# One pool of 2-KB slots for the early tiles, one-hot rows expanded on chip, query copies on VectorE

## The chip, the cores and the metric

The kernel runs on one core of a Trainium2 chip. The metric is the device time of one execution in microseconds. TensorE (PE) multiplies, VectorE (DVE), ScalarE (ACT) and GpSimd (POOL) work on tiles, SyncE (SP) and also ACT and POOL issue DMA transfers. Each engine takes its instructions in the order in which the program gives them and waits, at each, for what that instruction needs.

## The reference

Two layers follow each other: an attention that selects chunks of keys, and a two-layer MLP. The sizes are 4 batches, 8 heads, 768 positions, head size 64; the MLP takes 3072 tokens of 512 features through 2048.

```python
k_chunks = k.reshape(B, H, nc, chunk, D)              # chunk 32, nc 24
k_min, k_max = k_chunks.min(axis=3), k_chunks.max(axis=3)
ub = np.sum(np.maximum(q[:, :, :, None, :] * k_min[:, :, None, :, :],
                       q[:, :, :, None, :] * k_max[:, :, None, :, :]), axis=-1)
ub = np.where(pos[:, None] // chunk >= np.arange(nc)[None, :], ub, -1e9)
top_chunks = np.argsort(ub, axis=-1)[..., -6:]
scores = np.where(selected_and_causal, q @ k.T / np.sqrt(D), -1e9)
attn = softmax(scores)
x = (attn @ v).transpose(0, 2, 1, 3).reshape(B * S, H * D)
h = x @ w_in
out = (np.maximum(h, 0) + np.log1p(np.exp(-np.abs(h)))) @ w_out
```

Inputs and output are float32 in DRAM; the kernel multiplies in bfloat16.

## The kernel before, in words

The work is cut into 12 blocks of 256 queries (4 batches of 3 blocks each). Block n is prepared (`prep`), attended one pair of heads at a time (`attend`, four pairs), and sent through the MLP (`mlp_h`, then `mlp_y`).

*Preparation.* Keys and queries come with features on the partitions. `kx` holds the minimum and the maximum of every chunk of keys (L483, or L499 from the second batch on), `bd` (L516) places them so that one matmul against the positive part of the queries (`qp`) and one against the negative part (`qn`, both L554) gives the bound of every chunk (L575, L576). VectorE adds the causal mask (L582), finds the eight largest (L591) and writes for each query which chunks are below the sixth (L599, L602) to `mr`. This mask is transposed and becomes 32 further rows of the query operands: `qa` (64 feature rows and 32 mask rows, for the first head of a pair) and `qb` (for the second head). `qa`'s feature rows are copied from `qb` at L558: by POOL for the first three blocks, by VectorE afterwards.

*One-hot rows.* The key operands `ka` and `kb` have 32 rows that answer to the mask rows: one-hot rows, the same for every pair, which say to which chunk a key belongs and carry the large negative number. `c_ohb` builds them once in `ohb` (32 x 768): VectorE fills the tile (L317) and POOL cuts it with three selects (L305, L307, L309). A DMA issued by POOL (L324, in `background`) repeats them into `ka`, another into `kb`, 192 KB each, for each of the two buffers of `ka` and `kb`. The score matmul of L676 then adds the mask as it multiplies, and waits for these rows.

*Attention.* `attend` multiplies keys by queries (L676), ACT takes the exponential (L685), POOL clears what lies above the diagonal (L691), PE multiplies by v (L701), VectorE divides (L710, L722), and the result goes transposed into X (L730 and L735 for the first three blocks, a DMA transpose at L738 afterwards).

*The ramp.* The first three blocks (`NRAMP`, one batch) are handled otherwise than the rest, since nothing can hide them: PE transposes their keys and queries (L476, L535), ACT copies these from PSUM (L480, L539), and `ramp_loads` (L364) issues their 18 loads, two tiles each of k, q and v per block, 256 KB a tile, in pieces (L375 for k and q, L372 for v). Most are SP's; some of block 0's are ACT's. POOL casts their v tiles at L648. While PE has nothing to do in the ramp it multiplies zeros (L340)[...]; the planner puts these fillers in until its own time 30.

*Buffers.* A raw tile (`xf`, 128 x 512 float32, 2 KB a partition) has 8 buffers. After the ramp, casts go to `kq` (4 buffers of 2 KB, L445), DMA transposes to `kt` (2) and `mt` (2), and attention results to `oall` (2), each a pool of its own. After the ramp no more than four `xf` are in use (kind `l`).

*Weights.* w_in and w_out come as four chunks each by DMAs that POOL issues (L392, L395). `ORDER` says that they come after the loads of blocks 0, 1 and 2; `hold_pool` (L401) makes POOL wait for one tile named by `HOLD`, ("q", 1): block 2's second q tile. The loads of block 3 and later wait for the third w_out chunk (`LGATE`, a small DMA of SP's at L407).

*Who sets the order.* `Graph.schedule` is a planner that runs when the program is built. Every task has an engine, a duration, a priority and the tiles it reads and writes; the planner simulates the engines, the buffers and the DMA queues, and the order in which it starts the tasks is the fixed program order of every engine. In its DMA model (L155, L176) a queue gets a share by its packet size (`pkt`) plus 3 where others are busy. A task may have a second engine (`alt`), which the planner takes if it is free first; `port=True` keeps VectorE and POOL off each other's shared port. So any change of a duration, of a pool or of a priority can change the order everywhere.

Of the kernel before, what the change touches and what calls it, by code (L numbers as in the profile page):

```python
# [9 lines left out]
F32 = mybir.dt.float32  # L10
# [7 lines left out]
CH = 32  # L18
# [3 lines left out]
QB = 256  # L22
# [10 lines left out]
NRAMP = 3  # L33
WARM = 30.0
# [10 lines left out]
HOLD = ("q", 1)  # L45
# [3 lines left out]
PSUM_CAP = {"s": 3, "h": 3, "y": 2, "o": 2, "t": 3, "l": 4}  # L49


class Buf:
    def __init__(self, pool, kind=None):
        self.pool, self.kind, self.left, self.slot = pool, kind, 0, None
        self.held = {}
# [7 lines left out]
class Graph:  # L63
# [39 lines left out]
    def schedule(self):  # L103
# [44 lines left out]
        def flow(to):  # L148
            nonlocal moved
            while moved < to:  # L150
# [4 lines left out]
                slow = {id(q): q[0][2] if len(live) == 1 else q[0][2] + 3 for q in live}  # L155
# [16 lines left out]
        while True:  # L172
            nxt = events[0][0] if events else None
            live = [q for q in queues.values() if q]
            if live:
                total = sum(q[0][2] + (3 if len(live) > 1 else 0) for q in live)  # L176
                cand = moved + min(q[0][0] * total / q[0][2] for q in live)
                if nxt is None or cand < nxt:
                    nxt = cand
# [74 lines left out]
def build(nc, tiles):  # L254

    PE, AC, DV, PO, SP = nc and (nc.tensor, nc.scalar, nc.vector, nc.gpsimd, nc.sync) or (None,) * 5
    g = Graph({"ps": 8, "xf": 8, "kq": 4, "kt": 2, "qab": 6, "qpn": 4, "kx": 2, "ub": 2, "mr": 2,
               "mt": 2, "pt": 6, "st": 4, "oall": 2, "osb": 3, "x": 5, "g": 3, "e": 3, "yo": 2}, PSUM_CAP)
# [43 lines left out]

    def c_ohb():
        o = T("ohb")
        PO.affine_select(out=o, in_=o, compare_op=ALU.is_ge, fill=0.0, base=0,  # L305
                         channel_multiplier=-CH, pattern=[[1, S]])
        PO.affine_select(out=o, in_=o, compare_op=ALU.is_ge, fill=0.0, base=CH - 1,  # L307
                         channel_multiplier=CH, pattern=[[-1, S]])
        PO.affine_select(out=o, in_=o, compare_op=ALU.not_equal, fill=-1.0, base=-NCH,  # L309
                         channel_multiplier=1, pattern=[[0, S]])  # L310
# [5 lines left out]
    add("POOL", 0.45, c_identf, -10, w=["identf"], name="identf")  # L316
    add("DVE", 0.7, lambda: DV.memset(T("ohb"), NEG), -10, w=["ohb"], name="ohb0")  # L317
    add("DVE", 0.2, lambda: DV.memset(T("cmask"), 0.0), -9, w=["cmask"], name="cmask0")
    add("POOL", 2.5, c_ohb, -9, r=["ohb"], w=["ohb"], name="ohb")
    add("POOL", 0.35, c_cmask, -8, r=["cmask"], w=["cmask"], name="cmask")  # L320
    add("POOL", 0.45, c_ident, -7, w=["ident"], name="ident")
    def oh(which, i):
        dst = T("ka", i)[64:96] if which == "ka" else T("kb", i)[32:64]
        PO.dma_start(out=dst, in_=T("ohb").unsqueeze(1).to_broadcast([32, NP, S]))  # L324

    def background(i, pr, after):
# [576 lines left out]
```

## Time and profile before

| what | value |
|---|---|
| median of 4 runs | 265.21 us (265.0 to 265.6) |
| the profiled execution | 265.0 us |
| its span, first to last instruction | 263.3 us |
| TensorE's granted clock, mean | 0.996 |
| PE, ACT, DVE, POOL busy | 254.7, 202.4, 149.5, 91.8 us |
| DMA traffic | 40.03 MB, 152 GB/s over the span |
| zero matmuls (L340) | 134, 21.1 us |

The span is the time between the first and the last instruction; the execution has a little before and after it, 1.7 us here. "Busy" of PE is the union of pipelined matmuls, fillers included. A row of the profile's groups gives line, engine, operation, tiles (written<-read) with their shape and count, then busy time and the mean of one in ns, then the idle time of the engine before them and what ended it. A row of the view by windows gives busy time and number of instructions of each engine in that stretch, the granted clock, the DMA engines' share (it counts overlapping packets, so it passes 1) and the rate of the transfers. In a timeline, two instructions of one line that follow closely are merged ("x2").

### The profile page before, as it was taken

To read this page: it belongs to the slowest core of one execution; us is meant where nothing else is said; L and a number is where in the kernel's file an instruction comes from. 1 tells how busy PE (TensorE), PEld (TensorE's weight loads), DVE (VectorE), ACT (ScalarE), POOL (GpSimd) and SP (SyncE) were. 2 spreads that over 40 slices of the span, in tenths; PEclk is the share of its full clock that TensorE was granted. 3 is DMA by queue.
4 is the path that set the end of the run, shared out by engine and by line. 5 is a ranking of instruction groups with operands and counts; after the bars stand their busy time and mean duration, and the time that the engine had idled before them with its cause. 6 is when DMAs were issued, how large, how long until landed. Compare 5 with 4: busy or idle time off the path is not lost.

```text
span 263.3 us, 6794 instructions
## 1 busy us (share of the span) xinstructions
PE 254.7 (97%) x2594; PEld 191.8 (73%) x2594; DVE 149.5 (57%) x542; ACT 202.4 (77%) x366; POOL 91.8 (35%) x187
## 2 busy tenths in 40 slices
PE   8998999999979999999999999999999999999993
PEld 6797998777657677778668678668678778676751
DVE  7779676238389597729997766579263110210202
ACT  1795999987467977999679898949869789576650
POOL 7345763252327361346517172533201111100000
PEclk9999999999999999999999999999999999999998
DMA  8999999999994999999999997993213211130112
GB/s 158 212 200 210 178 208 196 207 184 223 217 239 98 211 256 179 247 196 235 153 212 224 198 239 147 208 194 80 40 47 79 41 44 40 39 83 0 42 40 80
DMA packets 121061, 40.03 MB, mean 152 GB/s; under 512 B 113668, under 2 KB 117764, under 8 KB 121028
## 3 DMA queue, kind: packets, MB, share of 16 engines
q1 hardware_dynamic: 113396, 33.83, 65.8%
q0 software_dynamic: 4480, 4.98, 11.2%
q10 hardware_dynamic: 3152, 0.79, 1.7%
q8 instruction: 20, 0.33, 0.5%
q14 instruction: 13, 0.11, 0.1%
HBM read 27.26 MB, written 6.29 MB: 127 GB/s over the span
## 4 chain that ended last, share of the span: by engine, by line
PE 80%; DVE 7%; DMA 6%; ACT 2%; issue 1%; SPq 1%; POOL 0%; DVEq 0%; ACTq 0%
PE ps L758 28%; PE ps L779 27%; PE ps L676 13%; PE ps L701 7%; DMA kt<-kq 3%; DMA xf<-in_v_dram 2%; PE ps L340 2%; DMA xf<-in_q_dram 1%; DVE qpn L554 1%; DVE kx L499 1%; PE ps L576 1%; SPq L438 1%; DVE bd L516 1%; ACT qab L539 1%; ACT kb L480 1%
## 5 line engine op out<-in xcount | busy, mean ns | idle before, releaser
L779 PE MATMUL ps<-w_out_sb,g 128*128 128x512 bf16 x384 | 106.3, 379 | 0.0
L758 PE MATMUL ps<-x,w_in_sb 128*128 128x256 bf16 x768 | 105.6, 272 | 0.2 <-DVE oall L722 0.2
L685 ACT ACTIVATE pt<-ps 128x512 bf16<-128x512 f32 (+1 forms) x192 | 92.9, 566 | 4.8 <-PE ps L676 4.1
L758 PEld LDWEIGHTS <-w_in_sb 128*128 128x128 bf16 x768 | 72.8, 98 | 24.7 <-issue 0.3
L764 ACT ACTIVATE e<-ps 128x512 f32<-128x512 f32 x96 | 57.3, 613 | 35.5 <-PE ps L758 35.1
L691 POOL TENSOR_SCALAR_AFFINE_SELECT pt<-pt 128x256 bf16<-128x256 bf16 x96 | 40.5, 428 | 102.8 <-ACT pt L685 102.8
L768 ACT ACTIVATE g<-e 128x1024 bf16<-128x1024 f32 x48 | 51.3, 1068 | 0.9
L779 PEld LDWEIGHTS <-g 128*128 128x128 bf16 x384 | 35.0, 98 | 13.9
L784 DVE COPY yo<-ps 128x512 f32<-128x512 f32 x24 | 16.5, 686 | 46.6 <-PE ps L779 46.4
L710 DVE RECIPROCAL st<-ps 128x4 f32<-128x4 f32 x48 | 8.4, 177 | 42.5 <-PE ps L701 29.6
L701 PEld LDWEIGHTS <-pt 128*128 128x128 bf16 x672 | 26.7, 97 | 5.3
L676 PE MATMUL ps<-qab,kb 128*128 128x256 bf16 x192 | 30.4, 259 | 0.2
L676 PE MATMUL ps<-qab,ka 96*128 96x256 bf16 x192 | 28.8, 258 | 1.5 <-DVE qab L641 1.5
L701 PE MATMUL ps<-v,pt 128*128 128x65 bf16 x672 | 28.3, 193 | 0.0
L445 POOL CAST kq<-xf 128x512 bf16<-128x512 f32 x36 | 22.4, 634 | 8.7 <-DMA xf<-in_k_dram 6.2
L499 DVE TENSOR_REDUCE kx<-kt 128x32 bf16<-128x1024 bf16 x18 | 21.5, 1211 | 4.9 <-DMA kt<-kq 4.8
L676 PEld LDWEIGHTS <-ka 96*128 96x128 bf16 x192 | 17.7, 97 | 8.2 <-issue 1.7
L340 PE MATMUL ps<-zero 128*128 128x256 bf16 x134 | 21.1, 289 | 1.1 <-DVE zero L344 1.1
L676 PEld LDWEIGHTS <-kb 128*128 128x128 bf16 x192 | 16.6, 97 | 5.5 <-DMA kb<-ohb 0.3
L443 POOL CAST v<-xf 128x512 bf16<-128x512 f32 x18 | 11.3, 631 | 15.6 <-DMA xf<-in_v_dram 15.5
L722 DVE TENSOR_TENSOR oall<-ps,st 128x256 bf16<-128x256 f32 x36 | 15.0, 420 | 0.8
L340 PEld LDWEIGHTS <-zero 128*128 128x128 bf16 x134 | 12.9, 104 | 2.9 <-DVE zero L344 1.1
(62 smaller groups left out, 186.4 us busy)
## 6 DMA issues: line engine op xcount, KB each, us to landing
out_dram<-yo SPq DMA_DIRECT2D x24, 256.0 KB, 2.9
xf<-in_v_dram SPq DMA_DIRECT2D x23, 256.0 KB, 5.1
xf<-in_k_dram SPq DMA_DIRECT2D x18, 256.0 KB, 4.3
xf<-in_q_dram SPq DMA_DIRECT2D x18, 256.0 KB, 4.8
w_in_sb<-in_moe_w_in_dram POOLq DMA_DIRECT2D x4, 512.0 KB, 8.5
w_out_sb<-in_moe_w_out_dram POOLq DMA_DIRECT2D x4, 512.0 KB, 13.0
xf<-in_k_dram SPq DMA_DIRECT2D x10, 128.0 KB, 5.2
xf<-in_q_dram SPq DMA_DIRECT2D x10, 128.0 KB, 3.9
```

The source lines that it names most:

```text
L340: PE.matmul(T(Fill)[:, 0:256], T("zero")[:, 0:128], T("zero"), start=True, stop=True)
L445: PO.tensor_copy(T(b_)[:, :, t], T(xf).rearrange("s (p c) -> s p c", p=NP))
L499: DV.tensor_reduce(T(kx)[:, m].rearrange("d p (t c) -> d p t c", t=NT), T(kt).rearrange("d (p t) (c s) -> d p t c s", t=NT, s=CH), axis=AX ...
L676: PE.matmul(T(sp)[:, z * QB:z * QB + QB - q0], kk[r0:r1, p, (j + z) * 128:(j + z + 1) * 128], qq[r0:r1, p, q0:QB], start=True, stop=True)
L685: AC.activation(T(pt)[:, j:j + 2].rearrange("k j c -> k (j c)")[:, 0:w], T(sp)[:, 0:w], ACT.Exp, scale=SCALE)
L691: PO.affine_select(out=diag, in_=diag, compare_op=ALU.is_ge, fill=0.0, base=0, channel_multiplier=-1, pattern=[[0, 2], [1, 128]])
L701: PE.matmul(o[:, u, h], T(pts[h])[:, j, c0:c0 + 128], T("v", i)[:, j, 2 * p + h, :], start=(j == 0), stop=(j == t0 + u))
L758: PE.matmul(o, T("w_in")[:, dt, ft * 128:(ft + 1) * 128], T(x)[:, dt], start=(dt == 0), stop=(dt == KDM - 1))
L764: AC.activation(T(e)[:, f2 * 2:f2 * 2 + 2].rearrange("f a s -> f (a s)"), T(hp), ACT.Exp)
L768: AC.activation(T(gb)[:, f4 * 4:(f4 + 1) * 4], T(e), ACT.Ln, bias=1.0)
L779: PE.matmul(T(y), T(gb)[:, f, u * 128:(u + 1) * 128], T("w_out")[:, f, :], start=(f == 0), stop=(f == KFF - 1))
L784: add("DVE", 0.6, lambda y=y, yo=yo: DV.tensor_copy(T(yo), T(y)), pr, r=[y], w=[yo], name=f"yo{n}")
```

## The change

Six things are edited.

- `xf`, `kq`, `kt`, `mt` and `oall` take their buffers from one pool `w2` of 18 slots of 2 KB; each sees a slot through its own view (`VIEWS`). Kinds keep the old numbers as caps for `kq`, `kt`, `mt`, `oall`, and 4 for the `xf` of later blocks. The ramp's `xf` have no cap.
- `HOLD` names block 2's first q tile.
- The one-hot rows are made of a small tile `eye` (32 x 24, POOL) which VectorE spreads over 32 columns for each chunk. For block 0's keys, ACT copies them into `ka` and `kb`, at a priority (`OHP`) between that of block 0's q and v loads; the DMAs of the first buffer carry blocks 1 and 2 alone. The score matmul waits for the rows of its own key block.
- The `qa` copies of the ramp go to VectorE.
- The v casts of the ramp may go to POOL or ACT.
- In the planner, a queue's share is by its packet size plus 1, the one-hot DMAs have another size and duration, and the set-up tasks other priorities.

```diff
+OHP = -98.5
+W2 = 18
...
-HOLD = ("q", 1)
+HOLD = ("q", 0)
...
-PSUM_CAP = {"s": 3, "h": 3, "y": 2, "o": 2, "t": 3, "l": 4}
+WIDE = {"xf", "kq", "kt", "mt", "oall"}
+PSUM_CAP = {"s": 3, "h": 3, "y": 2, "o": 2, "t": 3, "l": 4, "kq": 4, "kt": 2, "mt": 2, "oall": 2}
...
+        self.view = pool
+        if pool in WIDE:
+            pool, kind = "w2", kind or (pool if pool in PSUM_CAP else None)
...
-                slow = {id(q): q[0][2] if len(live) == 1 else q[0][2] + 3 for q in live}
+                slow = {id(q): q[0][2] if len(live) == 1 else q[0][2] + 1 for q in live}
...
-    g = Graph({"ps": 8, "xf": 8, "kq": 4, "kt": 2, "qab": 6, "qpn": 4, "kx": 2, "ub": 2, "mr": 2,
-               "mt": 2, "pt": 6, "st": 4, "oall": 2, "osb": 3, "x": 5, "g": 3, "e": 3, "yo": 2}, PSUM_CAP)
+    g = Graph({"ps": 8, "w2": W2, "qab": 6, "qpn": 4, "kx": 2, "ub": 2, "mr": 2,
+               "pt": 6, "st": 4, "osb": 3, "x": 5, "g": 3, "e": 3, "yo": 2}, PSUM_CAP)
...
+    def c_eye():
+        o = T("eye")
+        PO.memset(o, 0.0)
+        PO.affine_select(out=o, in_=o, compare_op=ALU.not_equal, fill=NEG, base=0,
+                         channel_multiplier=1, pattern=[[-1, NCH]])
+        PO.affine_select(out=o, in_=o, compare_op=ALU.not_equal, fill=-1.0, base=-NCH,
+                         channel_multiplier=1, pattern=[[0, NCH]])
+
     def c_ohb():
-        o = T("ohb")
...
+        DV.tensor_copy(T("ohb").rearrange("c (n s) -> c n s", s=CH), T("eye").unsqueeze(2).to_broadcast([32, NCH, CH]))
...
-    add("DVE", 0.7, lambda: DV.memset(T("ohb"), NEG), -10, w=["ohb"], name="ohb0")
-    add("POOL", 2.5, c_ohb, -9, r=["ohb"], w=["ohb"], name="ohb")
+    add("POOL", 0.5, c_eye, -12, w=["eye"], name="eye")
+    add("DVE", 0.86, c_ohb, -12, r=["eye"], w=["ohb"], name="ohb")
...
-    def oh(which, i):
-        dst = T("ka", i)[64:96] if which == "ka" else T("kb", i)[32:64]
-        PO.dma_start(out=dst, in_=T("ohb").unsqueeze(1).to_broadcast([32, NP, S]))
+    def oh(which, i, blks):
+        ks = slice(blks[0] * QB, (blks[-1] + 1) * QB)
+        dst = T("ka", i)[64:96, :, ks] if which == "ka" else T("kb", i)[32:64, :, ks]
+        return dst, T("ohb")[:, ks].unsqueeze(1).to_broadcast([32, NP, QB * len(blks)])
...
-            add("POOL", 0.6, lambda which=which: oh(which, i), pr, r=["ohb"], w=[(which + "c", i)],
-                name="oh" + which, after=after, dma=0.6, pkt=66, lat=0.7)
+            add("POOL", 0.6, lambda which=which: PO.dma_start(*oh(which, i, blks)), pr, r=["ohb"],
+                w=[(which + "c", i, k_) for k_ in blks], name="oh" + which, after=after, dma=0.8, pkt=200, lat=0.7)
...
-    background(0, -6, ())
+    for which in ("ka", "kb"):
+        add("ACT", 0.95, lambda which=which: AC.copy(*oh(which, 0, [0])), OHP, r=["ohb"], w=[(which + "c", 0, 0)],
+            name="oh" + which)
+    background(0, -6, (), [1, 2])
...
-            qe_, qd = ("POOL", 0.6) if ramp else ("DVE", 0.35)
-            add(qe_, qd, lambda sl=sl: (PO if ramp else DV).tensor_copy(T(qa)[0:64, sl], T(qb)[0:64, sl]), pr + 1.8,
+            add("DVE", 0.09 + 0.13 * len(hs), lambda sl=sl: DV.tensor_copy(T(qa)[0:64, sl], T(qb)[0:64, sl]), pr + 1.8,
                 r=[(qb, hh, z) for hh in hs for z in range(3)], w=[(qa, hh, 0) for hh in hs], port=True, name=f"qa{n}")
...
-                add("POOL", 0.55, lambda xv=xv, t=t: PO.tensor_copy(
-                    v_dst(n, t), T(xv).rearrange("s (h d) -> s h d", h=H)), pr + 2,
-                    r=[(xv, 0), (xv, 1)], w=[("v", i, blk * NT + t)], name=f"vc{n}")
+                def vc(eng, xv=xv, t=t):
+                    return lambda: (PO.tensor_copy if eng else AC.copy)(
+                        v_dst(n, t), T(xv).rearrange("s (h d) -> s h d", h=H))
+                add("POOL", 0.6, vc(1), pr + 2, r=[(xv, 0), (xv, 1)], w=[("v", i, blk * NT + t)], name=f"vc{n}",
+                    alt=("ACT", 0.52, vc(0)))
...
-                r = [(kn, i, j, hh), (kn, i, j + 1, hh), (kn + "c", i)] + ([("kb0", i)] if h else [])
+                r = [(kn, i, j, hh), (kn, i, j + 1, hh), (kn + "c", i, j // 2)] + ([("kb0", i)] if h else [])
...
-    background(1, BG, [landed["w_in", 3]])
+    background(1, BG, [landed["w_in", 3]], [0, 1, 2])
...
+VIEWS = {
+    "xf": lambda a: a.bitcast(F32),
+    "kq": lambda a: a.rearrange("s (p t c) -> s p t c", p=NP, t=NT),
+    "kt": lambda a: a.rearrange("d (j s) -> d j s", s=128),
+    "mt": lambda a: a.rearrange("d (p s) -> d p s", p=NP),
+    "oall": lambda a: a.rearrange("s (p t h d) -> s p t h d", p=NP, t=NT, h=2),
 }
```

## The prediction

> **What bounds the kernel now.** First the page's busy row and the filler's row, then the span cut in three (columns: length, busy time and instructions of PE, PEld, DVE, ACT and POOL, PE clock, DMA share, GB/s).
>
> ```profile
> PE 254.7 (97%) x2594; PEld 191.8 (73%) x2594; DVE 149.5 (57%) x542; ACT 202.4 (77%) x366; POOL 91.8 (35%) x187
> L340 PE MATMUL ps<-zero 128*128 128x256 bf16 x134 | 21.1, 289 | 1.1 <-DVE zero L344 1.1
> 0.00:31.00 31.00, 28.41 (x283) 24.38 (x284) 24.70 (x88) 20.09 (x40) 17.77 (x39) 1.00 1.07 191
> 31.00:259.30 228.30, 226.27 (x2313) 167.46 (x2311) 124.18 (x454) 182.35 (x327) 74.05 (x149) 1.00 0.76 147
> 259.30:263.30 4.00, 0.00 (x0) 0.00 (x0) 0.61 (x1) 0.00 (x0) 0.00 (x0) 0.76 0.34 131
> ```
>
> From 31 us to 259.3, PE lacks 2.03 us of being busy, 1.68 of it between 70 and 80. Before 31 it looks busy too, but 21.1 us is the zero matmul. So the span is a head of 31, a dense stretch, and a tail of 4 (last copy and store). The change adds and removes no real matmul: it can win only by starting the dense stretch earlier, and lose by opening holes in it.
>
> What ends the head? The same columns over the DMA stream, and the timelines of POOL, DVE and PE.
>
> ```profile
> 13.00:18.00 5.00, 5.00 (x64) 4.63 (x65) 3.78 (x14) 4.46 (x11) 2.68 (x7) 1.00 1.34 219
> 10.00:13.00 3.00, 2.91 (x32) 2.26 (x30) 2.17 (x14) 1.71 (x5) 1.79 (x3) 1.00 1.15 190
> 18.00:20.00 2.00, 2.00 (x25) 1.86 (x22) 1.82 (x7) 1.97 (x5) 0.68 (x3) 1.00 0.69 148
> 26.00:29.00 3.00, 3.00 (x33) 2.64 (x31) 2.97 (x9) 2.90 (x6) 3.00 (x5) 1.00 0.92 125
> 29.00:36.00 7.00, 7.00 (x103) 6.46 (x101) 3.37 (x13) 6.52 (x15) 5.67 (x12) 1.00 1.24 206
> ```
>
> ```profile
> 24.81 0.18 POOL L401 CAST scratch<-xf 1x1 bf16<-1x1 f32 x1 [2.81 <-DMA xf<-in_q_dram]
> 24.93 1.54 POOL L392 DMA_DIRECT2D w_in_sb<-in_moe_w_in_dram  x2
> ...
> 31.57 0.60 PE L758 MATMUL ps<-x,w_in_sb 128*128 128x256 bf16 x4
> ```
>
> The ramp's loads run at 219 GB/s, the weights at 206. POOL waits at L401 for block 2's second q tile and only then issues w_in. The first weight chunk needs 5.8 us to land (the shortest of that line's landings), 30.7, and the first MLP matmul runs at 31.57. X of block 0 was ready at 20.5 (its last copy, ACT L735 at 20.11, 0.37 long). The head is thus a DMA queue: 18 ramp tiles, then weights. The holes in it have names in SyncE's waits up to 32 us, for buffers not yet free:
>
> ```profile
> SPq L375 <- PE ps L576: 3.4, 1, 3.4
> SPq L375 <- POOL pt L691: 2.0, 1, 2.0
> ```
>
> Last, VectorE and GpSimd in the ramp:
>
> ```profile
> 19.84 1.64 DVE L516 COPY bd<-kx 64x64 bf16<-64x64 bf16 x2
> 19.92 0.61 POOL L558 COPY qab<-qab 64x512 bf16<-64x512 bf16 x1
> 20.84 0.60 POOL L558 COPY qab<-qab 64x512 bf16<-64x512 bf16 x1
> ```
>
> Two bd copies take 1.64 us while POOL copies qa; this copy's median is 0.178.
>
> **What the Trainium skill says.** "SBUF — State Buffer", section "SBUF: two separate sides": GpSimd and a VectorE operation in a two-port mode take an exclusive lock on one port pair, and the loser waits for the whole instruction. The bd row agrees: 1.46 for the longest, against 0.178. "DMA: Bandwidth & Descriptors", section "Queues, rings and completion order": each DMA engine goes round the queues that have work, packet by packet. So weights issued while ramp loads are queued get in between them; the trace of before hardly overlaps the two, and doesn't show the share.
>
> **The change, part by part.** Times are against the profiled execution (265.0, span 263.3, 1.7 around it).
>
> *Shared pool.* 18 ramp tiles fit 18 slots, so no ramp load waits for a buffer. Against 219 GB/s (206 for weights) the stream loses 3 x 29/219 = 0.40 us in 10:13, 2 x 71/219 = 0.65 in 18:20, 3 x 81/206 = 1.18 in 26:29. Sum 2.2. The last hole is partly the two block-2 v tiles issued late by SP (22.5), partly the late hold. I take all 2.2 as gained; at worst 1.2 (some of it may be the start-up of POOL's queue). In steady state the caps (4+4+2+2+2 = 14) are as before.
>
> *HOLD on q tile 0.* The hold opens a tile earlier: 262 kB/219 = 1.2 us. The weights then share with up to three ramp tiles; the bytes are the same. I take 0.4 for the first chunk (0 to 1.2), 0 for the end of the stream.
>
> *One-hot rows.* Block 0's rows go to two ACT copies, so the DMAs carry two thirds: 2 x 65.5 kB/219 = 0.6 us off the stream. The ACT copies have 1024 elements a partition: 1.07 each by the nearest row (L768, 128x1024, 1068 ns), 2.1 in all, inside ACT's idle 4.79 us before L480 at 6.88. Behind them on ACT stands block 0's second v load, issued at 4.80, perhaps 1 us later; its cast comes at 11.74 and the first AV matmul at 14.97, so about 2 us of cover. Gone, n=0 is later by up to 2.1, against X ready 11 us before use. Making the rows: POOL drops three selects of 0.815 (2.4) and adds a memset and two selects of 24 columns, under 0.3 each by the 128-column row (0.29); VectorE changes a 0.70 memset for a broadcast copy of 768, estimated 0.55 to 0.96 by "VectorE: DVE Perf Modes", section "The TRN2 errata — SBUF-src ops pay a fixed extra latency per instruction" (150 cycles plus 768, halved or not; no row of before has a broadcast copy). All before 5 us: nothing at the end.
>
> *qa copies to VectorE.* Six copies of 0.63 leave POOL. On VectorE I take 0.30 each (the qpn row of 128x512 is 0.316; 0.23 to 0.48 by the shortest qpn and the 64x1024 copy): 1.8, of which 1.2 falls before 26 us. It gives back 1.28 at bd and some 0.8 on four 128x256 qpn (0.43 mean against 0.226 shortest): net about -0.9 to +1.8, near zero taken, since DMA sets the end of the head. Queued behind these copies on VectorE are ub, max and mr of the same block.
>
> *v casts may go to ACT.* Up to six of 0.61 (L764's 128x512 row). Only four, 2.4 us, could fall where ACT is full: from 23 to 50 us it is idle 1.07.
>
> *The planner.* The queue penalty (3 to 1), durations and caps change the plan, so all static orders after the ramp may differ. The page can't price this; between -2.0 (the holes of the dense stretch closed) and +4; I take 0.
>
> Sum: first weight chunk 2.2 + 0.6 + 0.4 = 3.2 earlier (about 27.5, first MLP matmul at 28.4). The end of the weights, which releases the next loads (SP L407), is 2.8 earlier. PE's dense stretch needs both feeds, so the smaller counts: span 263.3 - 2.8 = 260.5, execution 262.2. The median of before is 0.2 above its profiled execution: 262.4.
>
> **Rivals.** A: *ScalarE becomes the bound.*
>
> ```profile
> 23.00:50.00 27.00, 27.00 (x348) 23.20 (x346) 17.40 (x85) 25.93 (x53) 14.12 (x27) 1.00 1.17 200
> ```
>
> ACT is as full as PE there. Only its idle stretch before L480 at 23.27 (2.78) can be filled; if two v casts also fall here (1.2) and the qa copies cost VectorE, and so block 1's first S, 0.7 net, 2.8 - 1.2 - 0.7 = 0.9 remains: 264.3. Against it: block 1's keys come earlier too.
>
> B: *the feed hole closes as well.* Between 70 and 80 us PE idles 1.68, waiting for block 4's kt. If the new plan orders SP's loads better, that and 0.3 besides goes: 260.4. For it: that hole is one load chain on SP; against: nothing in the diff speeds those transfers.
>
> C, *slower: SP's order.* SP issues loads, transposes and stores in one fixed order, and block 4's keys already come with no slack.
>
> ```profile
> 70.00:80.00 10.00, 8.32 (x85) 6.26 (x84) 7.51 (x20) 6.32 (x12) 3.28 (x7) 1.00 1.20 217
> ```
>
> A store put ahead of those loads, whose y tile is not finished, stops SP; store L788 waited 57.5 us in total, 11.6 at most, harmless late. A y tile is 16 matmuls of 512 columns, about 3.5 us of PE (two of the chain's 1.73 pieces of 8). One tile too early costs 3.5 and eats the gain; over 2.8 us it is slower. Two tiles, 7, less 2.8: about +4; I put the case at 267.5, between +0.7 and +4.
>
> D: *no change*, if the w_in landing is not what PE waits for: 265.2. Against it, X was ready 11 us before.
>
> **How the numbers follow.** Forecast 0.55 (own range 261.2 to 263.8), A 0.14, B 0.08, C 0.19, D 0.04. A change of 0.2% (0.53 us) is about what can be told here. Faster: forecast, B, most of A, 0.75; same: D and a bit of A, 0.06; slower 0.19. The range 259.8 to 266.6 takes in A, B, D and the near part of C; the worst of C and a low tail are left out.
>
> **What would show it.** No SP wait for PE or POOL in the ramp, and 219 GB/s held from 10 to 26 us. L401 ending near 22, the first L758 near 28.4, SP's L407 near 44, fewer fillers. No bd copy over 0.3 us in the ramp; block 0's S matmuls free of the kb<-ohb DMA. The dense stretch still about 228 long. I am wrong if L758 starts early and the hole at 70 to 80 has grown by as much (C), or if L758 starts early with ACT full and PE thin up to 50 (A), or if L401 still ends near 25.

## The result, and the profile after

The changed kernel takes 265.92 us (median; 264.43 to 269.12), the kernel before 264.99 in the same comparison: ratio 1.0037, 95% interval [1.0024, 1.005]. The ratio leaves out its two slowest executions (268.68 and 269.12), which lie over 1.5% above its fastest. It is slower by about 0.4%, where 262.4 was forecast. The profiled execution has a span of 264.0 us, against 263.3 before.

The page's busy row and the filler's row, then the span cut as in the prediction: head, dense stretch and tail, the DMA stream, and the stretches 23 to 50 and 70 to 140.

```profile
PE 254.7 (96%) x2593; PEld 191.9 (73%) x2593; DVE 146.2 (55%) x549; ACT 205.0 (78%) x369; POOL 85.0 (32%) x179
L355 PE MATMUL ps<-zero 128*128 128x256 bf16 x133 | 19.4, 287 | 1.1 <-DVE zero L325 1.1
```

```profile
31.00:260.00 229.00, 226.69 (x2310) 167.24 (x2308) 121.60 (x452) 182.37 (x329) 70.65 (x145) 1.00 0.71 144
260.00:264.00 4.00, 0.00 (x0) 0.00 (x0) 0.61 (x1) 0.00 (x0) 0.00 (x0) 1.00 0.35 131
10.00:13.00 3.00, 1.42 (x15) 1.26 (x16) 1.15 (x9) 2.91 (x7) 0.48 (x1) 1.00 1.15 260
13.00:18.00 5.00, 5.00 (x58) 4.25 (x56) 3.99 (x19) 4.00 (x9) 1.72 (x5) 1.00 1.11 248
18.00:20.00 2.00, 2.00 (x27) 1.85 (x25) 2.00 (x6) 1.94 (x5) 0.97 (x2) 1.00 0.57 129
23.00:26.00 3.00, 3.00 (x37) 2.81 (x35) 3.00 (x30) 2.55 (x5) 3.00 (x5) 1.00 0.71 97
23.00:50.00 27.00, 26.84 (x324) 22.97 (x322) 17.38 (x88) 26.11 (x53) 12.33 (x24) 1.00 1.15 199
70.00:80.00 10.00, 10.00 (x107) 7.75 (x106) 9.18 (x35) 7.72 (x15) 4.13 (x9) 1.00 1.06 198
80.00:90.00 10.00, 9.21 (x85) 6.20 (x84) 6.59 (x17) 7.70 (x14) 4.11 (x9) 1.00 0.81 142
120.00:140.00 20.00, 19.12 (x213) 13.77 (x211) 19.27 (x84) 14.31 (x29) 10.76 (x22) 1.00 1.04 212
```

Early loads run faster (248 to 260 GB/s), and the hole at 70 to 80 us is gone (PE 10.00 of 10). Two things are worse: PE is busy for only 1.42 of the 3 us from 10 to 13 (2.91 before), and it is thin at 80 to 90 and in 120 to 140. SyncE waits for no buffer in the ramp. Apart from the start of the program, its only wait up to 32 us is:

```profile
SPq L389 <- DMA w<-in_k_dram: 0.9, 1, 0.9
```

POOL's timeline around the hold (L415) and the first weights (start, length, "idle before"):

```profile
21.89 0.41 POOL L706 TENSOR_SCALAR_AFFINE_SELECT pt<-pt 128x256 bf16<-128x256 bf16 x1 [0.47 <-ACT pt L700]
22.25 0.18 POOL L415 CAST scratch<-w 1x1 bf16<-1x1 f32 x1
22.37 3.02 POOL L406 DMA_DIRECT2D w_in_sb<-in_moe_w_in_dram  x4
```

The DMA landings in the trace give four marks: w_in issued at 22.37 (24.93 before), first chunk landed at 28.54 (30.72), the last w_out chunk at 47.18 (49.78), SP's gate passed at 44.12 (46.70). The first MLP matmul runs at 29.99 (31.57). The hold did not wait for its tile: that tile's first piece had landed at 19.81, and the piece that the old hold reads at 20.84, while POOL came to the hold at 22.25, behind a select that had waited for ScalarE's exponential. So in this kernel it made no difference which of the two tiles the hold names.

So the stream did what was promised in direction and nearly in size. To see where the gain went I count the columns of all real matmuls (fillers left out) that have started by a moment, in units of 2400 columns (float32 columns count twice, and a matmul under 60 columns as 60); the whole is 229.35 in both kernels, and one unit is about one microsecond of the dense stretch (it advances 0.974 a microsecond from 140 to 255).

| by (us) | 15 | 31 | 60 | 80 | 90 | 130 | 135 | 255 |
|---|---|---|---|---|---|---|---|---|
| after minus before | -1.36 | +0.27 | -0.11 | +1.44 | +0.75 | +1.07 | -0.56 | -0.64 |

At 31 us, where the forecast had PE 2.8 ahead, it is 0.27 ahead: the first MLP matmuls come earlier, but there is less attention work done. The closed hole brings it to +1.44 at 80; it loses 1.6 between 130 and 135, and stays behind. Three questions follow: what holds the ramp back, why the earlier loads don't help later, and how much is the re-made plan.

ScalarE's timeline answers the first for a start. Of the kernel after, then of the kernel before:

```profile
3.65 0.38 ACTq L389 DMA_DIRECT2D w<-in_q_dram  x1
4.07 1.04 ACT L349 COPY ka<-ohb 32x1024 bf16<-32x1024 bf16 x1 [1.98 <-DMA w<-in_k_dram]
5.12 1.04 ACT L349 COPY kb<-ohb 32x1024 bf16<-32x1024 bf16 x1
8.99 0.38 ACTq L386 DMA_DIRECT2D w<-in_v_dram  x1
9.47 0.58 ACT L494 CAST ka<-ps 64x512 bf16<-64x512 f32 x1 [3.30 <-DMA w<-in_q_dram]
```

```profile
4.80 0.38 ACTq L372 DMA_DIRECT2D xf<-in_v_dram  x1
6.88 0.58 ACT L480 CAST ka<-ps 64x512 bf16<-64x512 f32 x1 [4.79 <-DVE kx L483]
```

The one-hot copies end at 6.16, in time. Block 0's second v load stands behind them, and it isn't issued until 8.99 (4.80 before), though its slot has been free from the start. The semaphore records of the trace say why. The loads of SP and ACT share eight semaphores, taken in turn in program order; a load waits until the transfer that had its semaphore last has landed. In the kernel before, the v load followed ACT's q load directly, and its turn fell on the semaphore of SP's second load (landed 4.78). After, seven loads of SP's stand between the two in the program, and the turn, having gone round once, falls on the semaphore of that q load itself: issued at 3.65, landed at 8.97. For 2.8 us ACT stands at a load, with the ka copy of L494 behind it. I call this *the stand*.

### The profile page after: what moved, and what is told of

Read it like the earlier page. It is cut to its first block, busy times and chain, and to the rows that moved or that the text cites. A ratio compares the mean times of both kernels' runs of the same rounds, so it can differ in the third digit from the quotient of the medians.

```text
span 264.0 us, 6800 instructions
## 1 busy us (share of the span) xinstructions
PE 254.7 (96%) x2593; PEld 191.9 (73%) x2593; DVE 146.2 (55%) x549; ACT 205.0 (78%) x369; POOL 85.0 (32%) x179
## 4 chain that ended last, share of the span: by engine, by line
PE 78%; DVE 10%; DMA 5%; ACT 4%; issue 2%; ACTq 0%; DVEq 0%
PE ps L794 26%; PE ps L773 26%; PE ps L691 13%; PE ps L716 7%; PE ps L355 4%; DVE kx L513 3%; DMA w<-in_q_dram 2%; ACT pt L700 2%; DMA w<-mr 1%; DMA w<-in_k_dram 1%; DVE mr L615 1%; DVE qpn L568 1%; DVE ub L604 1%; ACT e L779 1%; PE ps L589 1%
## 5 line engine op out<-in xcount | busy, mean ns | idle before, releaser
L799 DVE COPY yo<-ps 128x512 f32<-128x512 f32 x24 | 16.4, 685 | 48.2 <-PE ps L794 48.1
L716 PEld LDWEIGHTS <-pt 128*128 128x128 bf16 x672 | 26.6, 97 | 4.3
L716 PE MATMUL ps<-v,pt 128*128 128x65 bf16 x672 | 28.5, 193 | 0.0
L459 POOL CAST w<-w 128x512 bf16<-128x512 f32 x36 | 21.8, 625 | 11.4 <-DMA w<-in_k_dram 10.4
L513 DVE TENSOR_REDUCE kx<-w 128x32 bf16<-128x1024 bf16 x18 | 21.4, 1209 | 3.5 <-DMA w<-w 3.4
L355 PE MATMUL ps<-zero 128*128 128x256 bf16 x133 | 19.4, 287 | 1.1 <-DVE zero L325 1.1
L737 DVE TENSOR_TENSOR w<-ps,st 128x256 bf16<-128x256 f32 x36 | 15.1, 421 | 1.1
L457 POOL CAST v<-w 128x512 bf16<-128x512 f32 x18 | 11.0, 621 | 11.5 <-DMA w<-in_v_dram 11.5
```

The lines of the kernel that those rows point to most:

```text
L355: PE.matmul(T(Fill)[:, 0:256], T("zero")[:, 0:128], T("zero"), start=True, stop=True)
L459: PO.tensor_copy(T(b_)[:, :, t], T(xf).rearrange("s (p c) -> s p c", p=NP))
L513: DV.tensor_reduce(T(kx)[:, m].rearrange("d p (t c) -> d p t c", t=NT), T(kt).rearrange("d (p t) (c s) -> d p t c s", t=NT, s=CH), axis=AX ...
L716: PE.matmul(o[:, u, h], T(pts[h])[:, j, c0:c0 + 128], T("v", i)[:, j, 2 * p + h, :], start=(j == 0), stop=(j == t0 + u))
L799: add("DVE", 0.6, lambda y=y, yo=yo: DV.tensor_copy(T(yo), T(y)), pr, r=[y], w=[yo], name=f"yo{n}")
```

## The experiments

All are timed against the kernel before in five rounds. The edits act on the planner's finished order (`order`, a list of tasks that is then emitted) unless the diff says otherwise, and none leaves a part of the computation out. The diffs are shortened, some of them to words. A trace is of one execution; where two traces are compared, their landing times can differ by themselves: the first w_in chunk lands at 28.08 in one run below (e3) and at 26.45 in another (e7) that differs from it only from 50 us on.

### Parts of the change alone, in the kernel before

**The planner's price of a busy queue alone (e1).**

```diff
-q[0][2] + 3 for q in live          # both places
+q[0][2] + 1 for q in live
```

> The kernel before with one thing of the change alone: the planner's queue penalty 1 instead of 3. No operation is added or removed; only the order changes. Theory P (the plan decides: where the holes of the dense stretch fall moves the end by a microsecond either way, whatever the parts do): over 0.5 us away from before, with the holes between 60 and 140 us at other places. Theory S (the ramp decides, by ScalarE and its queue): within 0.5 us of before, since ScalarE's work is the same.

267.97 against 265.03, 1.0114 [1.007, 1.0158]. The re-made order alone costs some 1.1%, with PE 8.44 of 10 in 80 to 90 (9.82 before) and another hole at 150 to 160. My zero for the planner was no estimate.

**The slots alone (e2).** The order stays; early tiles take their buffer from 18 shared slots.

```diff
+    free = list(range(18))             # walk the order; each wide tile takes
+    b.slot = free.pop(0)               # the slot that came free first
```

> The kernel before, every engine's order kept, only the slots renamed: the five kinds of tiles share 18 slots, so no ramp load waits for a buffer. The forecast's step (2.2 us of holes in the DMA stream belong to the slots and the late hold, and pass to the end): the first w_in chunk lands 1 to 2 us before 30.7 and the time falls by 1 to 2 us. Theory S: w_in lands earlier, but PE and ScalarE are full from 31 us on, and the fillers are a fixed number, so the time falls by 0.5 us or less. If SyncE's waits were those of a window of outstanding DMAs and not of slots, w_in doesn't move at all.

265.98: 1.0018 [0.9994, 1.0043]. The first w_in lands at 30.04 instead of 30.72: 0.7 us, where 2.2 was counted for the slots. Even that need not be the slots' doing: in a run below that has the old buffers and the old hold (e13), it lands at 30.00. SyncE's issues hardly move; block 1's four q loads, before and in this run:

```profile
8.09 5.52 SPq L375 DMA_DIRECT2D xf<-in_q_dram  x4
8.08 5.37 SPq L378 DMA_DIRECT2D w<-in_q_dram  x4
```

The second of the four takes 3.69 us before and 3.50 here, and a later k load 2.52 and 2.51, although here no buffer is waited for. So what the waits showed as "for buffers" in the ramp had another limit beneath it. It isn't the turn of the eight semaphores either: the transfers that had the semaphores of these two loads last had landed at 8.26 and 13.84, before the issues began (8.80 and 15.25). What holds these issues stays open.

**The hold alone (e12).** The order stays; POOL's hold reads block 2's first q tile.

```diff
-tensor_copy(T("scratch")[0:1, 0:1], T(second q tile)[0:1, 0:1])
+tensor_copy(T("scratch")[0:1, 0:1], T(first q tile)[0:1, 0:1])
```

> The kernel before, every order kept, with POOL's hold on block 2's first q tile instead of the second. The forecast's step: the first w_in chunk lands 0.4 to 1.2 us before 30.7 and the time falls by up to that. Theory S (PE's and ScalarE's orders are fixed and both are full from 31 us on): w_in lands about 1 us earlier, the first MLP matmul 0.3 to 1 us, and the time stays within 0.4 us of before.

264.22: 0.9962 [0.9941, 0.9982], faster by 0.4%, but not as I had it. In the profiled execution the first w_in chunk lands no earlier (30.93), although issued 1.7 earlier (23.27): the last v tile of the ramp is still in the queue and lands at 31.25 instead of 28.36. That fits "DMA: Bandwidth & Descriptors" of the Trainium skill, section "Queues, rings and completion order", on queues served in turn. The first MLP matmul stays at 31.50. What moves is the feed of block 3: its first key tile lands at 51.73 instead of 53.13, its key transpose is issued at 53.82 instead of 55.04, and the hole at 70 to 80 shrinks by 1.0 (before: PE 8.32). Part of this may be chance, since with the old hold that tile lands at 52.57 (e13) and 52.65 (e2) in other runs; that the 0.4% comes from block 3's feed is likely, not shown.

```profile
70.00:80.00 10.00, 9.35 (x99) 7.22 (x98) 8.54 (x34) 7.44 (x14) 3.72 (x9) 1.00 1.15 208
```

### Undoing one thing in the changed kernel

**The v load first (e3).** Only block 0's second v load moves, ahead of ACT's two one-hot copies.

```diff
+    v = [t for t in order if t.name == "ldv01"][0]
+    order.remove(v)
+    order.insert(first_one_hot_copy_on_ACT, v)
```

> The changed kernel's order with one move: block 0's second v load stands on ScalarE's queue before the two one-hot copies, not behind them. Theory S: the load is issued near 4.8 us instead of 8.99, ScalarE's first ka copy runs near 7 instead of 9.47, block 0's first S matmul 2 to 2.6 us earlier, ScalarE has up to 2.6 us more to give before 31 us, and the time falls by 0.3 to 1.2 us. Theory P: block 0 is earlier, the holes stay, and the time stays within 0.3 us of the changed kernel.

264.19: 0.9967 [0.995, 0.9984]. One moved instruction turns +0.37% into -0.33%. ScalarE's timeline of this run:

```profile
4.28 0.37 ACTq L386 DMA_DIRECT2D w<-in_v_dram  x1
4.70 1.04 ACT L349 COPY ka<-ohb 32x1024 bf16<-32x1024 bf16 x1 [2.61 <-DMA w<-in_k_dram]
5.75 1.04 ACT L349 COPY kb<-ohb 32x1024 bf16<-32x1024 bf16 x1
6.82 0.58 ACT L494 CAST ka<-ps 64x512 bf16<-64x512 f32 x1
```

The one-hot copies themselves do fit: the ka copy comes at 6.82 (6.88 before). The move also lands the v tile earlier (10.30 for 12.47), but that is not what was missing: in the changed kernel block 0's v casts start at 12.52 and 12.84, and its first AV matmul (L716) runs at 17.23, behind the selects. The first MLP matmul is at 28.29, a little under the forecast 28.4, and PE is 1.87 units ahead at 31 us and 3.47 at 80. But by 135 the lead is 0.99, and in this profiled execution (span 263.3) nothing is left of it by 200 us; the median keeps 0.8 us of it.

**Other suspects in the changed kernel (e5, e6).** The last ten fillers dropped, which ran after w_in had landed; and, on top of the v load's move, two v casts taken off ScalarE:

```diff
-    order's last ten fillers                        # e5
-    v casts on ACT                                  # e6, e8
+    the same v casts on POOL
```

> The changed kernel's order without its last ten zero matmuls, those that ran between 28.5 and 30.1 us after the first weight chunk had landed (28.54). If the fixed number of fillers is what kept the earlier weights from PE: the first MLP matmul comes 1.1 us earlier and the time falls by 0.8 to 1.1 us. Theory S (ScalarE, full from about 20 to 50 us, sets the pace, and block 3's keys behind it): PE starts the MLP earlier, ScalarE doesn't, block 3's key transpose stays at 55, and the time falls by 0.4 us or less.

> The v load first, as in the run with that one move, and besides the two v casts that the plan gave to ScalarE (blocks 0 and 1, 0.62 and 0.65 us) done by POOL at the same places. Theory S: ScalarE gets 0.6 to 1.3 us back before 31 us, block 3's key transpose is 0.5 to 1 us earlier than the 53.3 of that run, and the time is 0.2 to 0.9 us below it. Theory P: no change over 0.2 us.

Fillers: 265.95, 1.004 [1.0025, 1.0055], as with them; the first MLP matmul comes at 29.30, 0.7 earlier, and the time doesn't follow. v casts: 264.38, 0.9959 [0.994, 0.9978], as without that edit (0.9967). The two casts, 0.64 us each on ACT, cost nothing that can be told.

**The feed of block 3 (e7, and with the v casts e8).** Its keys land 4.1 us earlier than before (the second tile at 50.15, before 54.27), and yet its key transpose is issued at the same time, 55.00 (55.04). POOL's timeline of the kernel after, then of the kernel before:

```profile
51.43 0.61 POOL L459 CAST w<-w 128x512 bf16<-128x512 f32 x1
54.01 0.41 POOL L706 TENSOR_SCALAR_AFFINE_SELECT pt<-pt 128x256 bf16<-128x256 bf16 x1 [1.97 <-ACT pt L700]
54.37 0.61 POOL L459 CAST w<-w 128x512 bf16<-128x512 f32 x1
```

```profile
52.20 0.41 POOL L691 TENSOR_SCALAR_AFFINE_SELECT pt<-pt 128x256 bf16<-128x256 bf16 x1 [1.45 <-ACT pt L685]
53.19 0.61 POOL L445 CAST kq<-xf 128x512 bf16<-128x512 f32 x1 [0.58 <-DMA xf<-in_k_dram]
54.32 0.61 POOL L445 CAST kq<-xf 128x512 bf16<-128x512 f32 x1 [0.52 <-DMA xf<-in_k_dram]
```

Before, the casts of the keys (L445) wait for DMA. After, the tiles are there, but a select of block 2 stands between the two casts and waits for ScalarE's exponential. ScalarE is busy for 26.11 of the 27 us from 23 to 50. So in this trace the earlier transfer is lost behind ScalarE. The test, on top of the v load's move:

```diff
+    second key cast of block 3 right after the first on POOL, ahead of that select
+    block 3's key transpose on SP moved up accordingly
```

> The v load first, and besides block 3's second key cast moved on POOL ahead of a diagonal select of block 2, which stood 1.97 us waiting for ScalarE's exponential, and block 3's key transpose right behind it on SyncE. Nothing changes on ScalarE, VectorE or PE. If that select is where the earlier weights and loads were lost (theory S, second half): the transpose is issued near 51 us instead of 53.3, block 3's chunk reductions near 57 instead of 59.2, and the time falls by 0.5 to 1.5 us against the run with the v load alone. If the feed of blocks 4 to 8 is set further down (by VectorE or the SyncE queue), block 3 is earlier and the time stays within 0.3 us.

> The changed kernel's order with all three moves: the v load first, the two v casts on POOL, block 3's key cast and transpose ahead. Theory S: the sum of the parts, 263 us or less against 265.0 of the kernel before and 265.9 of the changed one. Theory P: a hole elsewhere takes it back, and it is no faster than the v load alone (264.2).

The feed: 263.86, 0.9946 [0.9931, 0.9961], 0.2% below the v load's move alone, with intervals that overlap; so it isn't shown that this feed costs time. The transpose is issued at 51.0, but block 3's reductions on VectorE still start at 59.2, since VectorE's own order has the copy of a finished y tile (L799, 58.60) ahead. The part of the expectation that had them near 57 failed. With the v casts moved too: 263.94, 0.9957 [0.994, 0.9973]; nothing more.

### The hole at 130 to 135

PE's timeline of the kernel after shows the hole (last column: idle before, and its releaser):

```profile
132.88 0.20 PE L588 MATMUL ps<-bd,qpn 128*128 128x48 bf16 x1 [0.38 <-DVE qpn L568]
134.11 0.54 PE L691 MATMUL ps<-qab,ka 96*128 96x256 bf16 x4 [0.34 <-DVE qab L654]
```

Three runs tried to close it by order alone: four MLP steps ahead of block 8's bound matmuls (e4); VectorE's mask copies of block 7 ahead of block 8's preparation (e9); the same with everything of e8 (e10).

```diff
+    one h and three y steps moved ahead of ub8 on PE              # e4
+    ma7, mb7 moved ahead of bd8 on VectorE; ub8 on PE after S7    # e9, e10
```

> The changed kernel's order with four MLP steps (one of h for block 5, three of y for block 4, 1.7 us of PE) moved ahead of block 8's bound matmuls, where PE stood still at 132 to 134 us for VectorE. Theory P: PE's idle time there goes from about 1.4 us to under 0.4, and the time falls by 0.9 to 1.4, to below the kernel before. Theory S: the moved work is missed a few us later, while ScalarE's exponentials of block 7 come first, and the time falls by less than 0.4.

> The changed kernel's order with VectorE's two mask copies of block 7 (L654, L656) moved ahead of block 8's bd, qp and qn, and block 8's bound matmuls moved behind the first S matmuls of block 7 on PE. In the changed kernel PE stood at 132.4 to 134.1 us for these. If VectorE's order is the cause of that hole: block 7's first S matmul near 132.5 instead of 134.1, the hole under 0.5 us, and the time 0.6 to 1.4 us below the changed kernel, that is 264.5 to 265.3. If the hole is only where PE's lead over the attention feed is used up: it moves by a few us and the time stays within 0.3 us of the changed kernel.

> The same move added to the three of the run before (v load first, v casts on POOL, block 3's keys ahead; 263.9). If VectorE's order makes the hole: 262.6 to 263.3. If PE's lead is used up there anyway: 263.6 to 264.2.

e4: 265.89, 1.003 [1.0015, 1.0044]; the hole at 132 to 134 is filled, and PE is as far behind at 140 as without it. e9: 267.3, 1.0084 [1.0052, 1.0115]; the mask copy comes at 131.8 instead of 133.2, PE's work at 135 and 140 is the same. e10: 264.87, 1.0008 [0.998, 1.0035], worse than e8. The profiled execution of e9 is its fastest (266.04), so why its median is 1.4 us above the changed kernel isn't seen in it. The hole isn't a fault of two neighbours in the order. My reading, which no run shows by itself, is that PE has used up the work that doesn't depend on block 7's mask, and that VectorE, full there (19.27 of 20 us), decides.

### Is it the stand by itself?

The kernel before was given the stand. A first attempt let the shared slots and SP's order bring it about:

```diff
+    order: ldv01 after three SP loads            # e11, with e2's slots
```

> The kernel before with renamed slots (the run with slots only, 266.0), and block 0's second v load put behind SyncE's loads of block 1's keys in the program; no engine's own order differs from that run. If the load's wait, for a DMA semaphore that eight loads share in turn and that still belongs to an earlier load, is what costs the changed kernel its ramp: ScalarE issues the load near 8.9 us instead of 4.74, its first ka copy comes 2 to 2.6 us later, and the time is 1.0 to 2.0 us above 266.0. If block 0's delay is absorbed: within 0.4 us of 266.0.

The stand did not arise: the v load was issued at 4.75, and ACT's first key copy ran at 6.87. 265.38, 1.0008 [0.9992, 1.0023] is thus little more than a second measurement of the slots alone, and inconclusive for its question. The second attempt (e13) put a tiny copy on ACT that reads the q half which lands at 8.97:

```diff
+    wait = add("ACT", ..., AC.copy(scratch[0:1, 0:8], q_half[0:1, 256:264]), r=[(q, 1)])
+    order.insert(ACT's first ka copy, wait)
```

> The kernel before, with one instruction added on ScalarE ahead of its first key copy of block 0: a copy of eight numbers of the first row of a q half that ScalarE itself fetched, into an unused tile. It makes ScalarE stand until that q half has landed, near 8.5 to 9.0 us, as the v load does in the changed kernel; everything else, plan and slots and one-hot rows, is that of the kernel before. Theory (ScalarE's stand is what cost the changed kernel its start): first key copy near 9 instead of 6.9, and 266.0 to 266.9 against 265.0. Rival (before 31 us TensorE waits for weights anyway, so the stand is absorbed, and the changed kernel loses elsewhere): within 0.4 of 265.0.

```profile
8.98 0.20 ACT L826 CAST scratch<-xf 1x8 bf16<-1x8 f32 x1 [6.88 <-DMA xf<-in_q_dram]
9.08 0.57 ACT L481 CAST ka<-ps 64x512 bf16<-64x512 f32 x1
```

The stand is there, the first MLP matmul is 1.4 later (33.0), and the kernel takes 265.67 against 265.24: 1.0009 [0.9984, 1.0034]. The theory's 266.0 to 266.9 failed. But the median stands for no execution. Six of the fourteen, with a mean granted clock of 0.999 or 1.0, take 264.05 to 264.69; the other eight, with 0.993 to 0.997, take 265.59 to 266.52. The kernel before doesn't split like this in the same comparison (medians 265.14 for 17 executions at 0.999 or above, 265.55 for the other 11). So in the first group the stand costs nothing; what sets the second apart, beyond its lower clock, no trace shows. The trace is of the first group (264.41), and POOL shows what absorbs the stand there:

```profile
53.64 0.41 POOL L692 TENSOR_SCALAR_AFFINE_SELECT pt<-pt 128x256 bf16<-128x256 bf16 x1 [1.45 <-ACT pt L686]
53.99 1.17 POOL L446 CAST kq<-xf 128x512 bf16<-128x512 f32 x2
```

The selects come 1.44 later (53.64 for 52.20), but the casts had been waiting for DMA anyway and now run back to back; block 3's transpose is issued at 55.19 against 55.04. PE, late at 31 us, meets the feed of block 3 on time: the hole at 70 to 80 takes the lateness (PE 9.95 of 10 there, 8.32 before). If that is the reason, the stand must cost once the hold has brought the tiles forward (e16):

```diff
+    e12's hold and e13's wait together
```

> The kernel before with two edits at once: POOL's hold on block 2's first q tile (alone 264.22 against 264.99) and the instruction that makes ScalarE stand until about 9 us (alone 265.67 against 265.24). Theory: the stand by itself is free in the kernel before because POOL's two key casts of block 3 wait for their tile until 54.3 there, longer than the stand pushes POOL's selects back; with the hold the tiles land earlier, the selects become what the casts wait for, and the stand eats the gain: block 3's key transpose again near 55.2 and 265.0 to 265.7. Rival (the stand is free whatever feeds block 3): 264.0 to 264.6, with the transpose near 53.8.

266.29 against 264.93: 1.0055 [1.0035, 1.0075], where the hold alone gave 0.9962. The direction is as expected, and the size is larger (2.1 us by the medians, where 0.8 to 1.5 was expected). But the trace doesn't show the theory at work. POOL at the hold (L826), then the windows around 12 us:

```profile
24.83 0.23 POOL L826 CAST scratch<-xf 1x1 bf16<-1x1 f32 x1
9.00:12.00 3.00, 0.70 (x9) 0.44 (x8) 0.78 (x3) 2.79 (x6) 0.66 (x1) 1.00 1.18 221
12.00:15.00 3.00, 3.00 (x19) 2.33 (x17) 1.62 (x9) 1.04 (x3) 1.54 (x3) 0.53 1.36 211
```

POOL comes to the hold at 24.83, when both q tiles have landed (the last piece at 24.71). The hold brings nothing forward: w_in is issued at 25.01 (24.93 before), and block 3's second key tile lands at 54.72 (54.27 before); its key transpose is issued at 56.50 (53.82 with the hold alone). And TensorE idles for 2.3 of the 3 us from 9 to 12, after which its granted clock is at half from 12.19 to 15.60. With the stand alone it idles for 1.6 us there, and the traced execution keeps its clock. This may be why the first MLP matmul slips to 34.3 here, by more than the 1.4 of the stand alone. The clock isn't the whole cost: seven of the nine executions have a mean of 0.990 to 0.994, but the two at 1.0 take 266.32 and 265.83. Neither of these was traced, so what the stand costs beside the hold is measured, and why stays open. In the changed kernel the clock is not the cause: 3 of its 41 executions lie below 0.996.

### How much is the plan?

The changed kernel with the planner's price back at 3 (e14), then the same with the v load first (e15), then also with e7's feed (e17):

```diff
-q[0][2] + 1 for q in live          # both places of the changed kernel
+q[0][2] + 3 for q in live
```

> The changed kernel with the planner's price for two running queues back at 3 in both places, so that only the order of the work differs from the changed kernel. Theory that the plan costs the changed kernel about as much as the price alone cost the kernel before (3 us there): 263 to 264.5. Rival (the price fits one plan by luck and says nothing of another): within 0.6 of 265.9 or slower.

> The changed kernel with the price back at 3 and block 0's second v load ahead of the one-hot copies on ScalarE. If ScalarE's stand and the plan are two separate losses: 1.5 to 2 us faster than the kernel with the price alone put back, so 261.5 to 263. If the early start is used up later whatever the plan: 263.8 to 264.5, as with the v load's move alone (264.19).

> The changed kernel with the planner's price at 3, block 0's second v load ahead of the one-hot copies, and block 3's second key cast ahead of a select on POOL with its transpose after it: the three edits that helped, together. With the price at 3 block 3's key transpose is planned late (55.7 with the v load moved), so if the feed of block 3 still binds: 262.0 to 262.8. Rival (hole at 70 to 80 is down to 0.8 us, the rest is set by later blocks): 262.8 to 263.3, as without the feed's edit (263.01).

| | v load behind the copies | v load first | v load first, feed |
|---|---|---|---|
| price 1 | 1.0037 [1.0024, 1.005] | 0.9967 [0.995, 0.9984] | 0.9946 [0.9931, 0.9961] |
| price 3 | 1.0013 [0.9996, 1.0031] | 0.9934 [0.9899, 0.9969] | 0.9916 [0.9887, 0.9945] |

In microseconds: 265.57, 263.01 and 262.52 for the second row. Within each row the v load gives 0.7 to 0.8%; price 3 is ahead in each column by 0.2 to 0.3%, but the two intervals of each column overlap, so this is not settled. The windows of the run with price 3 alone show that the hole of 130 to 135 belongs to the plan: it is gone (19.84 of 20), and another stands in 80 to 90.

```profile
120.00:140.00 20.00, 19.84 (x225) 15.17 (x226) 19.51 (x77) 15.83 (x31) 10.50 (x21) 1.00 0.81 193
80.00:90.00 10.00, 8.17 (x65) 5.43 (x65) 4.84 (x16) 7.01 (x14) 4.47 (x9) 1.00 0.81 124
```

With the v load first it is this hole that shrinks, from 1.83 to 0.25 (0.78 is then missing in 70 to 80):

```profile
120.00:140.00 20.00, 19.84 (x218) 15.12 (x219) 19.26 (x84) 15.83 (x31) 10.46 (x20) 1.00 0.81 192
80.00:90.00 10.00, 9.75 (x97) 6.89 (x97) 6.10 (x15) 7.57 (x16) 3.67 (x8) 1.00 0.74 165
```

The last run, 262.52 against 264.93, is the fastest of all and beats both kernels: the whole change with one planner constant left as it was, one load moved ahead of two copies, and one cast ahead of a select. Its gain over the run without the feed edit (0.2%) is within both intervals.

## Why the prediction was wrong

It forecast 262.4 and 75% for faster; the kernel is 0.4% slower. Step by step:

- *Shared pool, hold, one-hot DMA: 3.2 us for the first weight chunk, 2.8 for the end of the stream.* Measured 2.2 and 2.6. The end was near right (SP's gate at 44.12, forecast 44). For the first chunk two terms were too large. The hole that I read as 1.18 us lost in 26 to 29 moves with the weights: 97 GB/s in 23 to 26, right after their issue, so it may be the start of POOL's queue; the step had named that as its doubt. The hole at 18 to 20 wasn't closed at all (129 GB/s, 148 before). I had read SyncE's waits as waits for buffers; the run with the slots alone waits for none, and its long issues are nearly as long as before. Its one trace has the first chunk 0.7 earlier, no more than a run with the old buffers. The hold's 0.4 was misplaced: alone it brought the first chunk nothing, and in the changed kernel POOL came to the hold after both tiles' first pieces had landed. That the hold ended near 22, as forecast, is luck.
- *The one-hot copies "inside ACT's idle 4.79 us", with the v load "perhaps 1 us later".* **This step failed, and it decides the sign.** The copies took 1.04 each, as costed, and fitted. The v load behind them was 4.2 later, for a reason that the sum didn't contain: its issue had to wait for a semaphore. I had named the instruction and asked when its data would be needed, never what its issue waits for or what stands behind it on ACT. The stand is 2.8 us of ScalarE at a time when the ramp's chain passes through ScalarE; undone, the same kernel is 0.7% faster. The Trainium skill, "DMA: Bandwidth & Descriptors", section "Anatomy of one DMA — SWDGE (gpsimd) path", says that a semaphore is waited for by the issuing sequencer before dispatch. The section is about GpSimd's transfers; the trace agrees for ScalarE's, 6.16 to 8.99 on its queue. I hadn't used it.
- *The cover "X ready 11 us before use".* It is true for block 0's X and the wrong cover. A late ramp doesn't delay the first MLP matmul much (29.99); attention work is missing at 31 us, and with ScalarE nearly full (26.11 of the 27 us from 23 to 50) POOL's selects and block 3's casts are late. By 31 us 2.5 of the missing 3.5 us of span are gone (0.27 ahead instead of 2.8). Moving the v load gives 1.6 of them back (1.87 ahead). The rest isn't the first MLP matmul, which then came at 28.29, no later than forecast; it stays open. The run with the stand put into the kernel before shows that such lateness can be absorbed; on what that depends isn't shown.
- *qa copies, bd, rows of the one-hot.* Sizes right. qa takes 0.34 on VectorE (0.30 taken); bd's mean falls from 0.389 to 0.228, as the exclusive port of the Trainium skill's "SBUF — State Buffer", section "SBUF: two separate sides", had it; the broadcast copy took 0.48 for an estimate of 0.55 to 0.96. None matters for the end.
- *v casts on ACT "up to 2.4".* Two of 0.64 went there; moving them back changes nothing.
- *The planner "I take 0".* Mis-sized: 1.1% alone in the kernel before; the 0.2 to 0.3% in the changed kernel is not settled. The bounds (-2 to +4 us) held it, but a cost of zero for a re-made order of 6800 instructions was a choice without a reason. With the price at 3 and the v load first, the kernel takes 263.01, inside the forecast's own range (261.2 to 263.8).
- *Rivals.* A (ScalarE the bound) has the right engine and the wrong ending: 26.11 of 27 busy from 23 to 50, and block 3's feed behind it, but it ended at 264.3, with a third of the gain kept. B happened, the hole at 70 to 80 closed, worth 1.9 by the count of columns (-0.43 at 70 us, +1.44 at 80), and most of it was lost at 130 to 135. C's sign came true by another mechanism: no store in front of loads shows up, and the waits in the holes are for VectorE's mask copies. D fell as I had put it: w_in's landing did move PE's first MLP matmul. But that matmul did not decide.

Of what should have shown the forecast wrong, the case "PE starts early and the dense stretch has a new hole" is what the page shows (226.69 busy of 229.00), at another place than I had looked.

## What to carry to other kernels

When work is put ahead of a DMA issue on a compute engine, ask what the issue itself waits for (a shared semaphore's last owner, here a transfer that landed 2.8 us after the copies had ended) and which instruction stands behind it, not only when the data are needed. A gain at the start of a dense stretch can be lost later: here with the v load first, a lead of 2.45 units at 130 us was 0.99 at 135. So find the first hole after the start, and see whether its feed waits for a transfer or for an engine, before the gain is counted. Look at the granted clock of each execution before a small ratio is read as one effect. Where a planner makes the order, a changed constant is a change of its own: try it alone.

## What the runs showed of the hardware

- SP's and ACT's loads of the ramp take eight semaphores in one common turn, so the place of a load among the loads of the *other* engine decided whether ACT stood for 2.8 us or not at all. This is how the program is built, rather than the chip, but only the trace shows it.
- A stand of ScalarE until about 9 us cost 0.1% [-0.2, 0.3] in the kernel before and 0.7 to 0.8% in the changed kernel: the price of a wait isn't a property of the wait.
- TensorE's granted clock was at half for 3.41 us in two traces before the tail: from 12.19 with hold and stand (e16), after 2.3 us of idling in 9 to 12, and from 77.44 with the slots alone (e2), after 1.65 us of idling from 73.98. It was not in the changed kernel after 1.84 us of idling from 9.74, nor in the kernel before after 1.53 us from 74.32.
- A transfer issued 1.7 us earlier landed 0.2 later (w_in in e12: 23.27 to 30.93, before 24.93 to 30.72), beside one v tile still in flight, which itself came 2.9 later; one trace each. The same transfer, issued at 20.68 and 20.37, landed at 28.08 and 26.45 in e3 and e7.
- Two issues of SyncE took 3.50 and 2.51 us in the run with the slots alone, with their semaphores free and no buffer to wait for; 0.5 us is usual there. What held them isn't shown.
- A VectorE copy that spreads 32 x 24 to 32 x 768 took 0.48 us, against 0.70 for the memset and three POOL selects of 0.815 that made the same rows before.
